# A state-space scan and a channel mixer on one core: decays folded into B and C, small matmuls packed into the array

## The chip, the cores and the metric

The kernel runs on one core of a Trainium2 chip. The metric is the device time of one execution in microseconds (us). The kernel before takes 431.71 us, the median of three runs (431.37 to 436.95). In a core, TensorE (PE) multiplies matrices: it loads a stationary operand (PEld) and streams a moving one past it, with results in PSUM, which has eight banks. VectorE (DVE), ScalarE (ACT) and GpSimd (POOL) work element by element, and SyncE's queue (SPq) issues the DMAs. An engine executes its own instructions in order and waits on semaphores for the others.

## The reference

Two blocks, one after the other. The first is a scan over 768 tokens, in 4 batches and 8 heads, with 32 channels per head (d) and 16 state numbers (n):

```
log_a = np.log(np.clip(a, 1e-06, 1.0))
for c in range(nc):                                  # chunks of 32 tokens
    cum = np.cumsum(la, axis=-1)
    L = np.exp(cum[:, :, :, None] - cum[:, :, None, :]) * causal
    M = np.einsum('bhin,bhjn->bhij', Cc, Bc) * L
    y_intra = np.einsum('bhij,bhjd->bhid', M, xc)
    y_inter = np.einsum('bhin,bhnd->bhid', Cc, state) * np.exp(cum)[:, :, :, None]
    y[:, :, sl] = y_intra + y_inter
    Bx = np.einsum('bhjn,bhjd->bhjnd', Bc, xc) * np.exp(cum[:, :, -1:] - cum)[:, :, :, None, None]
    state = np.exp(np.sum(la, axis=-1))[:, :, None, None] * state + np.sum(Bx, axis=2)
```

The second is a mixer on y as x, of shape (4, 768, 256), with U (768 x 32), V (32 x 768), w_ch1 (256 x 1024) and w_ch2 (1024 x 256), all four given as float64:

```
h = x.transpose(0, 2, 1) @ U @ V
u = x + h.transpose(0, 2, 1)
return u + np.maximum(u @ w_ch1, 0.0) @ w_ch2
```

## The kernel before

Everything is fp32. The scan goes in chunks of 128 tokens, six to a batch, with all eight heads at once. `scan_front` (lines 206 to 249) prepares a chunk. GpSimd spreads log a into `lau`; TensorE transposes B, C times its decay, and C (L225); C is masked into four copies (CTm, L230) so that one matmul with 64 rows and 512 columns gives C B^T of four heads (L248, two per chunk, one for each half of the rows, each into a PSUM bank of its own). The decay matrix L comes from a matmul of `lau` with a 0/1 triangle (L239, two per chunk of 512 columns), an exp on ScalarE (L240) and a mask on GpSimd (L241); VectorE multiplies both into M (L249). `scan_back` (lines 251 to 280) makes y, token-major, in one bank: one matmul of the state with the decayed C (L259) and eight matmuls, one per head, with M as the stationary operand and 32 moving columns (L262). Then come the sum of new states, as one 128 x 256 matmul (L269), its masking on VectorE (L272), the old state's decay on GpSimd (L276) and their sum (L279).

The mixer of a batch is a list of pieces (lines 283 to 342). `project` makes U^T y in six matmuls of 256 columns (L292) and VectorE copies the result to pT (L294). `u_channel_major` (four times) transposes three blocks of y (L299) and adds V's product of 32 rows and 384 columns in the same bank (L302), which VectorE copies (L304). `up` (16 times) is two matmuls of 384 columns (L311) and a relu on VectorE or ScalarE (L314, L316). `down` (six times) is a V product (L323), eight matmuls of 256 columns (L325) and an addition of y on VectorE (L327). A DMA writes three token blocks at a time.

The weights' float64 words are taken apart on chip by `to_fp32` (lines 164 to 200): eleven tiles (U one, V two, w1 four, w2 four), each with seven operations on VectorE (lines 179 to 191, and L196) and two on GpSimd (L194, L198). Their words land in six buffers. The DMA queue brings the first batch's B, C and x first, then the weights, then the other batches.

Order of the work: the loop at the end gives the scan of batch 0 the weight tiles as pieces, and the scan of every later batch the mixer of the batch before; the last mixer runs alone. Written order is only a wish here: a scheduler places the instructions on each engine, TensorE included. An instruction that stands behind a waiting one on its engine waits too.

Of the kernel before, what the change touches and what calls it, by code (L numbers as in the profile page):

```python
# [10 lines left out]
INT32 = mybir.dt.int32  # L11
WCOLS = 512
NWORDS = 6
AF = mybir.ActivationFunctionType
ALU = mybir.AluOpType


@with_exitstack
def kernel(
# [26 lines left out]
    NC = S // P  # L46
    DM = NH * D
# [6 lines left out]
    assert NH * N == P and DM == 2 * P and HS % P == 0  # L54

    const = ctx.enter_context(tc.tile_pool(name="const", bufs=1))
    raw = ctx.enter_context(tc.tile_pool(name="raw", bufs=NB * NC))
# [5 lines left out]
    BANKS = {"misc": 1, "diff": 2, "g": 2, "y": 1, "mlp": 2}  # L63
# [11 lines left out]
    x_sb, bc_sb = {}, {}  # L75

    def load(b, c):
        sl = ts(c, P)
        bc = bc_sb[b, c] = raw.tile([P, 2, NH, N], FP32, tag="bc", name="bc")
        nc.sync.dma_start(out=bc[:, 0], in_=B[b, :, sl, :].rearrange("h s n -> s h n"))  # L80
        nc.sync.dma_start(out=bc[:, 1], in_=C[b, :, sl, :].rearrange("h s n -> s h n"))
        xt = x_sb[b, c] = raw.tile([P, NH, D], FP32, tag="x", name="x")
        nc.sync.dma_start(out=xt, in_=x[b, :, sl, :].rearrange("h s d -> s h d"))

    for c in range(NC):
        load(0, c)
# [3 lines left out]
    V_sb = const.tile([RK, S], FP32)  # L90
# [4 lines left out]
    def load_words(dst, src):  # L95
        """dst [p, i, j], and its float64 words in DRAM, [p, i, (j two)]."""
        p, i, j = dst.shape
        t = raw.tile([P, 2 * WCOLS], INT32, tag="words", name="words", bufs=NWORDS)
        t = t[:p, :2 * i * j].rearrange("p (i j) -> p i j", i=i)
        nc.sync.dma_start(out=t, in_=src)  # L100
        weights.append((dst, t))
# [3 lines left out]
    for k in range(2):  # L105
        load_words(V_sb[:, None, ts(k, S // 2)], V2[:, None, ts(k, S)])
    for c in range(NCB):
        for k in range(DF // WCOLS):
            load_words(w1[:, c, None, ts(k, WCOLS)],
                       w12[ts(c, P), None, ts(k, 2 * WCOLS)])  # L110
# [4 lines left out]
    for b in range(1, NB):  # L115
        for c in range(NC):
            load(b, c)

# [5 lines left out]
    upto = const.tile([P, P], FP32)  # L124
    nc.gpsimd.affine_select(
        out=upto, in_=ones, pattern=[[1, P]], compare_op=ALU.is_ge, fill=0.0,
        base=0, channel_multiplier=-1)
    after = const.tile([P, P], FP32)
    nc.gpsimd.affine_select(
        out=after, in_=ones, pattern=[[-1, P]], compare_op=ALU.is_ge, fill=0.0,  # L130
        base=-1, channel_multiplier=1)
    hmask = const.tile([P, NH], FP32)
    nc.gpsimd.affine_select(
        out=hmask, in_=ones[:, :NH], pattern=[[-N, NH]], compare_op=ALU.is_ge, fill=0.0,
        base=0, channel_multiplier=1)
    nc.gpsimd.affine_select(
        out=hmask, in_=hmask, pattern=[[N, NH]], compare_op=ALU.is_ge, fill=0.0,
        base=N - 1, channel_multiplier=-1)
    tmask = const.tile([P, 4], FP32)
    nc.vector.tensor_tensor(out=tmask, in0=hmask[:, 0:4], in1=hmask[:, 4:8], op=ALU.add)  # L140

# [1 line left out]
    la = const.tile([P, NB, NC, NH], FP32)  # L143
    R = NB * NH * NC // 2
    la_ps = bank("misc", 2, R)
# [11 lines left out]
    decay = const.tile([P, 3, NB, NC, NH], FP32)  # L157
    for k, tri in enumerate((upto, after, ones)):
        d = bank("diff", NB * NC * NH)
        nc.tensor.matmul(out=d, lhsT=tri, rhs=la_flat, start=True, stop=True)  # L160
        nc.scalar.activation(decay[:, k].rearrange("p b c h -> p (b c h)"), d, AF.Exp)

# [1 line left out]
    def to_fp32(dst, words):  # L164
        """dst = the float32 nearest to each float64, of which words hold the low and high half.

        A float64 is +-2^(e - 1023) (1 + h 2^-20 + l 2^-52): the factor in brackets is rounded to
        float32 once, and the power, clamped to float32's range, put together as bits.
        """
        p, i, j = dst.shape  # L170
        words = words.rearrange("p i (j two) -> p (i j) two", two=2)
# [218 lines left out]
```

## Time and profile before

| | us |
|---|---|
| median of three runs | 431.71 |
| runs | 431.37, 431.71, 436.95 |
| span of the profiled execution | 433.4 |
| PE busy in it | 400.8 (92%), 1552 matmul records |
| DVE busy | 163.3 (38%) |
| ACT busy, POOL busy | 64.2, 91.7 |

The profiled execution's own time is its span of 433.4 us from the first to the last instruction, 1.7 us above the median of the runs. An fp32 matmul appears as two records of a load and two of a matmul, a transpose as one of each; a few records can be missing. A matmul's time in a row includes its drain, so that in a dense stretch the distance from start to start is what it costs. TensorE's clock has two levels, 1.2 and 2.4 GHz; PEclk is the granted share of the higher one.

### The profile page before, as it was taken

How to read it: one execution, taken by the hardware profiler on the slowest of the kernel's cores; microseconds unless marked ns; L12 is line 12 of the kernel's file. 1: busy time of each engine (PE TensorE's matmuls, PEld its weight loads, DVE VectorE, ACT ScalarE, POOL GpSimd, SP SyncE). 2: the span in 40 equal slices, each digit the busy share in tenths (PEclk: the TensorE clock that was granted, in tenths of full speed). 3: DMA queues.
4: the chain of work that ended last, by engine and by line, in shares of the span. 5: the costliest groups of instructions: out<-in, count | busy, mean ns of one | idle time of the engine just before them, and what ended most of it. 6: DMA issues, size and time to landing. Idle time of an engine off the chain costs nothing.

```text
span 433.4 us, 4009 instructions
## 1 busy us (share of the span) xinstructions
PE 400.8 (92%) x1552; PEld 250.8 (58%) x1552; DVE 163.3 (38%) x315; ACT 64.2 (15%) x134; POOL 91.7 (21%) x120
## 2 busy tenths in 40 slices
PE   6297975959999999999999999999999999999996
PEld 3063542545356775575558656755666667657664
DVE  2279789675333224313341343132323230211110
ACT  4112101101111112110220122011301210010000
POOL 4347746333100202202220222022111100000000
PEclk9769688575589999999999999996999999979999
DMA  7965999500000010010000100000000100100101
GB/s 96 207 154 103 159 117 116 66 2 0 0 1 2 0 37 2 0 38 0 0 2 0 36 2 0 5 32 1 2 0 0 38 0 0 38 0 0 38 0 36
DMA packets 80850, 14.37 MB, mean 33 GB/s; under 512 B 75968, under 2 KB 79232, under 8 KB 80832
## 3 DMA queue, kind: packets, MB, share of 16 engines
q1 hardware_dynamic: 80832, 14.13, 18.0%
q8 instruction: 12, 0.20, 0.2%
q14 instruction: 6, 0.05, 0.0%
HBM read 10.98 MB, written 3.15 MB: 33 GB/s over the span
## 4 chain that ended last, share of the span: by engine, by line
PE 85%; DVE 8%; SPq 3%; issue 2%; DMA 1%; POOL 1%; ACT 0%; DVEq 0%
PE mlp L311 20%; PE mlp L325 20%; PE y L262 11%; PE diff L239 7%; PE g L248 7%; PE mlp L302 4%; PE mlp L323 3%; PE misc L269 2%; PE y L259 2%; PE mlp L292 2%; PE mlp L299 2%; PE misc L225 2%; DVE f L196 1%; DVE M L249 1%; DVE cdec L215 1%
## 5 line engine op out<-in xcount | busy, mean ns | idle before, releaser
L311 PE MATMUL mlp<-uT,w 128*128 128x384 f32 x256 | 92.7, 508 | 0.0
L325 PE MATMUL mlp<-w,gT 128*128 128x256 f32 x384 | 90.1, 386 | 0.0
L325 PEld LDWEIGHTS mlp<-w,gT 128*128 128x128 f32 x384 | 70.7, 190 | 18.8 <-issue 10.2
L311 PEld LDWEIGHTS mlp<-uT,w 128*128 128x128 f32 x256 | 48.9, 197 | 42.3 <-issue 16.0
L262 PEld LDWEIGHTS y<-x,M 128*128 128x128 f32 x384 | 56.2, 226 | 5.3 <-issue 3.1
L262 PE MATMUL y<-x,M 128*128 128x32 f32 x384 | 55.0, 302 | 0.0
L239 PE MATMUL diff<-lau,after 128*128 128x512 f32 x96 | 54.8, 675 | 0.1
L241 POOL TENSOR_SCALAR_AFFINE_SELECT L<-L 128x512 f32<-128x512 f32 x48 | 33.7, 706 | 82.7 <-ACT L L240 82.6
L249 DVE TENSOR_TENSOR M<-g,L 128x512 f32<-128x512 f32 x48 | 31.1, 685 | 35.6 <-PE g L248 32.3
L327 DVE TENSOR_TENSOR o<-mlp,ytok 128x256 f32<-128x256 f32 x24 | 10.2, 424 | 84.3 <-PE mlp L325 84.3
L276 POOL TENSOR_TENSOR kept<-state,decay 128x256 f32<-128x256 f32 x16 | 11.3, 708 | 142.5 <-DVE state L279 113.9
L248 PE MATMUL g<-CTm,T 64*128 64x512 f32 x96 | 32.5, 760 | 7.9 <-DVE CTm L230 7.9
L240 ACT ACTIVATE L<-diff 128x512 f32<-128x512 f32 x48 | 28.2, 597 | 47.0 <-PE diff L239 27.1
L314 DVE TENSOR_SCALAR gT<-mlp 128x384 f32<-128x384 f32 x32 | 17.8, 555 | 42.0 <-PE mlp L311 41.9
L316 ACT ACTIVATE gT<-mlp 128x384 f32<-128x384 f32 x32 | 15.7, 491 | 116.5 <-PE mlp L311 116.5
L265 ACT COPY ytok<-y 128x256 f32<-128x256 f32 x24 | 9.0, 373 | 153.2 <-PE y L262 153.2
L210 POOL TENSOR_SCALAR_AFFINE_SELECT lau<-la 128x1024 f32<-128x1024 f32 x24 | 27.2, 1136 | 6.1 <-PE diff L239 3.5
L225 PE MATMUL misc<-ident,bc 128*128 128x128 f32 x48 | 13.8, 306 | 13.9 <-DVE state L272 13.2
L239 PEld LDWEIGHTS diff<-lau,after 128*128 128x128 f32 x96 | 18.9, 220 | 10.6 <-issue 6.8
L272 DVE TENSOR_TENSOR state<-misc,hmask 128x256 f32<-128x256 f32 x20 | 8.4, 422 | 42.6 <-PE misc L269 42.6
L225 PEld LDWEIGHTS misc<-ident,bc 128*128 128x128 f32 x48 | 7.6, 159 | 26.7 <-DVE state L272 22.3
L248 PEld LDWEIGHTS g<-CTm,T 64*128 64x128 f32 x96 | 8.5, 216 | 21.6 <-DVE CTm L230 17.1
(57 smaller groups left out, 285.0 us busy)
## 6 DMA issues: line engine op xcount, KB each, us to landing
words<-in_moe_w_ch_dram SPq DMA_DIRECT2D x8, 512.0 KB, 3.8
x<-in_x_dram SPq DMA_DIRECT2D x24, 128.0 KB, 3.4
out_dram<-o SPq DMA_DIRECT2D x8, 384.0 KB, 2.5
bc<-in_B_dram SPq DMA_DIRECT2D x24, 64.0 KB, 3.1
bc<-in_C_dram SPq DMA_DIRECT2D x24, 64.0 KB, 2.8
words<-in_moe_U_dram SPq DMA_DIRECT2D x1, 192.0 KB, 4.0
words<-in_moe_V_dram SPq DMA_DIRECT2D x2, 96.0 KB, 3.8
a_sb<-in_a_dram SPq DMA_DIRECT2D x1, 96.0 KB, 2.1
```

What stands on the lines that cost most here:

```text
L210: nc.gpsimd.affine_select(out=lau, in_=la[:, b, c, :, None].to_broadcast([P, NH, P]), pattern=[[0, NH], [1, P]], compare_op=ALU.is_ge, fil ...
L225: nc.tensor.transpose(out=tp[:, k], in_=src.rearrange("p h n -> p (h n)"), identity=ident)
L239: nc.tensor.matmul(out=d, lhsT=after, rhs=lau[:, hs], start=True, stop=True)
L240: nc.scalar.activation(L[:, hs], d, AF.Exp)
L241: nc.gpsimd.affine_select(out=L[:, hs], in_=L[:, hs], pattern=[[0, 4], [1, P]], compare_op=ALU.is_ge, fill=0.0, base=0, channel_multiplier=-1)
L248: nc.tensor.matmul(out=g, lhsT=T[r, 0], rhs=CTm[r], start=True, stop=True)
L249: nc.vector.tensor_tensor(out=M[:, hs], in0=g, in1=L[:, hs], op=ALU.mult)
L262: nc.tensor.matmul(out=y[:, ts(h, D)], lhsT=s["M"][:, h], rhs=xt[:, h], start=(c == 0 and h == 0), stop=True, skip_group_check=True)
L302: nc.tensor.matmul(out=t, lhsT=pT[:, ts(n, P)], rhs=V_sb[:, ts(k, HS)], start=False, stop=True, skip_group_check=True)
L311: nc.tensor.matmul(out=g, lhsT=w1[:, n, ts(m, P)], rhs=uT[:, n, ts(k, HS)], start=(n == 0), stop=(n == NCB - 1))
L314: nc.vector.tensor_relu(gT[k][:, m], g)
L325: nc.tensor.matmul(out=o, lhsT=gT[k][:, m, ts(j, P)], rhs=w2[:, m], start=False, stop=(m == NM - 1))
```

## The change

The scan goes in pairs of chunks. Its decays are factored: exp(cum_i - cum_j) becomes a factor on C's row i times one on B's row j, relative to one of two reference tokens in the chunk (FB and FC, made once for all chunks; `v` counts the references). `prep` forms the scaled B and C of a pair (Bs on VectorE, Cs and bd on GpSimd), each head taking 32 numbers (2 x 16); `turn` transposes them, four transposes a chunk; L, `lau`, the exp and their masks are gone, and M is C B^T with a causal bit mask. `gram` (C B^T) packs four heads into four 32-row tiles of the array, with a PSUM bank each; `state` and the inner part of `ychannel` pack four heads into four 32-column tiles; `project` does the same with four token blocks of U, whose result stands in four row groups for which V is loaded four times over (V4). y is made channel-major, which is what the mixer's up-product takes; `ytokens` transposes it to token-major for `project` alone. `mixed` adds h to y in place with one matmul of 128 rows; `down` starts from two transposes of u in place of V's product and y's addition. The PSUM banks are 3 for everything (w), 4 for C B^T, 1 for y. `to_fp32` has five operations on VectorE, one on ScalarE and one on GpSimd. TensorE's order is the written one (`manual_schedule`); the other engines' orders still come from the scheduler.

The core of the diff:

```
-        for k in range(2):
-            hs = slice(4 * k, 4 * k + 4)
-            d = bank("diff", 4, P)
-            nc.tensor.matmul(out=d, lhsT=after, rhs=lau[:, hs], start=True, stop=True)
-            nc.scalar.activation(L[:, hs], d, AF.Exp)
...
-            g = bank("g", 4, P)
-            nc.tensor.matmul(out=g, lhsT=T[r, 0], rhs=CTm[r], start=True, stop=True)
-            nc.vector.tensor_tensor(out=M[:, hs], in0=g, in1=L[:, hs], op=ALU.mult)
...
+    def turn(k, c):
+        tp = bank("w", 4, P)
+        for i, name in enumerate(("Bs", "Cs")):
+            flat = s[name].rearrange("p h v n -> p (h v n)")
+            for g in range(2):
+                nc.tensor.transpose(out=tp[:, 2 * i + g], in_=flat[:, ts(2 * c + g, P)],
+                                    identity=ident)
...
+    def gram(k):
+        g_ps = bank("g", 4, 2, 2, P)
+        for c in range(2):
+            T = s["T", c]
+            for g in range(2):
+                for r in range(4):
+                    rows = ts(r, Q)
+                    nc.tensor.matmul(out=g_ps[:, r, c, g], lhsT=T[rows, g], rhs=T[rows, 2 + g],
+                                     start=True, stop=True, skip_group_check=True)
+        for c in range(2):
+            nc.vector.tensor_tensor(
+                out=M[:, :, c].bitcast(INT32), in0=g_ps[:, :, c].bitcast(INT32),
+                in1=causal[:, None, None, :].to_broadcast(sh), op=ALU.bitwise_and)
+    def state(k):
...
+        for c in range(n):
+            for g in range(2):
+                for r in range(4):
+                    h = 4 * g + r
+                    nc.tensor.matmul(
+                        out=A[ts(r, Q), c, g],
+                        lhsT=s["bd"][:, c * NH + h].rearrange("p v n -> p (v n)"),
+                        rhs=x_sb[k][:, c, h], start=r not in first, stop=True,
+                        skip_group_check=True)
...
+    def ychannel(k):
...
+                nc.tensor.matmul(
+                    out=y[:, c, g], lhsT=wide[:, g].rearrange("p r d -> p (r d)"),
+                    rhs=s["T", c][:, 2 + g], start=fresh, stop=False, skip_group_check=True)
...
+        for c in range(2):
+            for g in range(2):
+                for r in range(4):
+                    nc.tensor.matmul(
+                        out=y[ts(r, Q), c, g], lhsT=x_sb[k][:, c, 4 * g + r],
+                        rhs=s["M"][:, r, c, g], start=False, stop=True, skip_group_check=True)
...
         def project():
+            for c in range(NC):
+                nc.tensor.matmul(out=p[ts(c % 4, Q)], lhsT=U_sb[:, c], rhs=ytok[b][:, c],
+                                 start=(c < 4), stop=(c >= NC - 4), skip_group_check=True)
+            nc.scalar.copy(out=pT, in_=p)
...
+        def mixed(k, n):
+            h = bank("w", HS)
+            nc.tensor.matmul(out=h, lhsT=pT[:, ts(n, P)], rhs=V4[:, ts(k, HS)],
+                             start=True, stop=True)
+            u = uT[:, n, ts(k, HS)]
+            nc.vector.tensor_tensor(out=u, in0=h, in1=u, op=ALU.add)
...
         def down(k, j):
-            nc.tensor.matmul(out=o, lhsT=V_sb[:, ts(t, P)], rhs=pT, start=True, stop=False)
+            for n in range(NCB):
+                nc.tensor.matmul(out=o[:, ts(n, P)], lhsT=uT[:, n, ts(HT * k + j, P)], rhs=ident,
+                                 is_transpose=True, start=(n == 0), stop=False,
+                                 skip_group_check=True)
...
-            nc.vector.tensor_tensor(out=hold[k][:, j], in0=o, in1=xs[:, t], op=ALU.add)
+            nc.scalar.copy(out=hold[k][:, j], in_=o)
...
+    with tc.manual_schedule(engines={PE}):
...
+            if k + 2 < last:
+                prep(k + 2)
+            if k + 1 < last:
+                turn(k + 1, 0)
+                some(parts[0])
+                turn(k + 1, 1)
...
+            some(parts[1])
+            ychannel(k)
+            if k + 1 < last:
+                state(k + 1)
+                gram(k + 1)
+            some(parts[2])
```

`some(n)` takes the next n pieces: weight tiles in batch 0, pieces of the mixer of the batch before in the later ones (22 for three pairs; `project` and the four `mixed` run at the start of a batch).

TensorE's order in the middle of a batch, before: L259 and L262 are y of a chunk, L269 its states, L239 and L225 belong to the next chunk, L248 is its C B^T, and L311 and L325 are the mixer's up and down.

```order
L259 MATMUL y<-state,T 128x256
L262 MATMUL y<-x,M 128x32 x8
L269 MATMUL misc<-x,bdec 128x256
L239 MATMUL diff<-lau,after 128x512
L225 MATMUL misc<-ident,bc 128x128
L225 MATMUL misc<-ident,cdec 128x128
L225 MATMUL misc<-ident,bc 128x128
L239 MATMUL diff<-lau,after 128x512
L311 MATMUL mlp<-uT,w_104 128x384
L248 MATMUL g<-CTm,T 128x512 x2
L311 MATMUL mlp<-uT,w_104 128x384 x7
```

The same place after: L298 is `turn`, L368 and L375 are `ychannel`, L331 `state`, L311 `gram`, L386 `ytokens`, L419 the mixer's up.

```order
L298 MATMUL w<-ident,Bs 128x128 x2
L298 MATMUL w<-ident,Cs 128x128 x2
L419 MATMUL w<-yT,w_98 128x384 x4
L368 MATMUL y<-T,wide 128x128 x4
L375 MATMUL y<-M,x 32x128 x16
L331 MATMUL w<-x,bd_260 32x32 x16
L311 MATMUL g<-T 128x128 x16
L431 MATMUL w<-ident,yT 128x128 x2
L435 MATMUL w<-w_99,gT 128x256 x8
```

The two 512-column products of a chunk are gone, and the scan's part of a pair now stands as three runs of 16 small matmuls in a row, with the mixer's pieces before and behind them and no longer between them.

VectorE's order in the first batch, before: L179 to L196 take weight tiles apart, L249 is M, and L272 evacuates the sum of states.

```order
L249 TENSOR_TENSOR M<-g,L 128x512 x2
L185 SCALAR_TENSOR_TENSOR power<-words,power 128x512
L196 SCALAR_TENSOR_TENSOR f<-l,f 128x512
L179 TENSOR_SCALAR power<-words 128x512
L188 TENSOR_SCALAR h<-words 128x512
L181 TENSOR_SCALAR power<-power 128x512
L191 TENSOR_SCALAR l<-words 128x512
L183 TENSOR_SCALAR power<-power 128x512
L196 SCALAR_TENSOR_TENSOR f<-l,f 128x512
L185 SCALAR_TENSOR_TENSOR power<-words,power 128x512
L272 TENSOR_TENSOR state<-misc,hmask 128x256
```

After, in the same stage: L237 to L248 take weight tiles apart, L345 adds the states, L316 masks M, L388 copies y's tokens.

```order
L275 TENSOR_TENSOR Bs<-bc,FB 128x512
L248 SCALAR_TENSOR_TENSOR rest<-words,power 128x512
L345 SCALAR_TENSOR_TENSOR S<-S,kept,w 128x32 x2
L316 TENSOR_TENSOR M<-g,causal 128x4x256 x2
L237 TENSOR_SCALAR e<-words 128x512
L244 TENSOR_SCALAR top<-words 128x512
L237 TENSOR_SCALAR e<-words 128x512
L244 TENSOR_SCALAR top<-words 128x512
L241 SCALAR_TENSOR_TENSOR power<-words,power 128x512
L388 COPY ytok<-w 128x512
```

Weight tiles still stand between the scan's operations on VectorE, two at a time, and the states are now added behind fewer of them.

## Rows read from the trace of the kernel before

**Rows 1.** The page: its first line, and the granted clock in 40 slices.

```profile
span 433.4 us, 4009 instructions
PEclk9769688575589999999999999996999999979999
```

**Rows 2.** Stretches: us, busy time (and instructions) of PE, PEld, DVE, ACT, POOL, PEclk, DMA share, GB/s.

```profile
80.00:90.00 10.00, 6.15 (x12) 1.60 (x8) 8.43 (x11) 1.08 (x2) 4.93 (x5) 0.76 0.18 22
...
100.00:110.00 10.00, 10.00 (x27) 5.85 (x28) 5.13 (x9) 1.84 (x4) 3.94 (x4) 0.50 0.00 0
...
140.00:160.00 20.00, 20.00 (x89) 14.01 (x88) 5.45 (x11) 2.40 (x6) 2.89 (x4) 1.00 0.06 20
```

**Rows 3.** Timeline of the front: start, duration, engine, line, operation [idle before <-releaser].

```profile
18.58 0.26 DVE L179 TENSOR_SCALAR power<-words 128x192 int32<-128x192 int32 x1 [8.75 <-DMA words<-in_moe_U_dram]
...
73.03 0.41 DVE L272 TENSOR_TENSOR state<-misc,hmask 128x256 f32<-128x256 f32 x1
...
81.47 1.22 PE L269 MATMUL misc<-x,bdec 128*128 128x256 f32 x2
...
90.11 0.41 DVE L272 TENSOR_TENSOR state<-misc,hmask 128x256 f32<-128x256 f32 x1
...
102.99 0.41 DVE L294 COPY pT<-mlp 32x256 f32<-32x256 f32 x1
```

**Rows 4.** Timeline of PE, one chunk of the scan in the settled stage.

```profile
145.62 0.59 PE L259 MATMUL y<-state,T 128*128 128x256 f32 x2
146.06 1.87 PE L262 MATMUL y<-x,M 128*128 128x32 f32 x16
...
149.13 0.27 PE L225 MATMUL misc<-ident,bc 128*128 128x128 f32 x1
149.24 0.27 PE L225 MATMUL misc<-ident,cdec 128*128 128x128 f32 x1
...
150.41 0.69 PE L323 MATMUL mlp<-pT,V_sb 32*128 32x256 f32 x2
...
151.67 1.13 PE L248 MATMUL g<-CTm,T 64*128 64x512 f32 x4
```

**Rows 5.** Timeline of PE, mixer: channel-major steps of batch 1, up and down of batch 3.

```profile
201.15 0.55 PE L299 MATMUL mlp<-ident,ytok 128*128 128x128 f32 x3
...
202.47 0.55 PE L299 MATMUL mlp<-ident,ytok 128*128 128x128 f32 x3
...
405.89 10.48 PE L311 MATMUL mlp<-uT,w 128*128 128x384 f32 x32
416.30 0.69 PE L323 MATMUL mlp<-pT,V_sb 32*128 32x256 f32 x2
416.93 3.72 PE L325 MATMUL mlp<-w,gT 128*128 128x256 f32 x16
420.58 0.69 PE L323 MATMUL mlp<-pT,V_sb 32*128 32x256 f32 x2
```

**Rows 6.** Timeline: a load and its matmul behind a wait, and out of the queue.

```profile
66.57 0.50 PEld L239 LDWEIGHTS diff<-lau,after 128*128 128x128 f32 x2 [0.86 <-issue]
66.60 2.48 PE L239 MATMUL diff<-lau,after 128*128 128x512 f32 x4
...
79.45 0.51 PEld L248 LDWEIGHTS g<-CTm,T 64*128 64x128 f32 x4
79.46 2.08 PE L248 MATMUL g<-CTm,T 64*128 64x512 f32 x4
```

**Rows 7.** Groups by line and form on VectorE: count | busy us, mean ns of one | idle before.

```profile
L249 DVE TENSOR_TENSOR M<-g,L 128x512 f32<-128x512 f32 x48 | 31.1, 685 | 35.6 <-PE g L248 32.3 <-POOL L L241 3.3
...
L185 DVE SCALAR_TENSOR_TENSOR power<-words,power 128x512 int32<-128x512 int32 x8 | 6.3, 790 | 0.0
...
L179 DVE TENSOR_SCALAR power<-words 128x512 int32<-128x512 int32 x8 | 5.1, 634 | 0.0
```

**Rows 8.** Stretches, columns as in rows 2, behind the last batch's scan.

```profile
378.00:381.00 3.00, 3.00 (x7) 1.31 (x7) 1.12 (x2) 0.00 (x0) 0.00 (x0) 0.55 0.00 0
```

More of the change, by code (lines that the diff above doesn't have):

```diff
@@ L46 @@
     NC = S // P
+    NPR = NC // 2
     DM = NH * D
@@ L113 @@
                    w22[m * P:(m + 2) * P].rearrange("(m p) d -> p m d", p=P))
-    for b in range(1, NB):
-        for c in range(NC):
-            load(b, c)
+    for k in range(NPR, NB * NPR):
+        load(k)
     ident = const.tile([P, P], FP32)
@@ L123 @@
     nc.vector.memset(ones, 1.0)
[L124 to L140, printed above, removed]
+    def triangle(name, out, pattern, base, mult, in_=None):
+        nc.gpsimd.affine_select(
+            out=out, in_=ones[:, :out.free_size()] if in_ is None else in_, pattern=pattern,
+            compare_op=ALU.is_ge, fill=0.0, base=base, channel_multiplier=mult)
+        return out
@@ new lines @@
+    upto = triangle("upto", const.tile([P, P], FP32, name="upto"), [[1, P]], 0, -1)
+    after = triangle("after", const.tile([P, P], FP32, name="after"), [[-1, P]], -1, 1)
+    low = [triangle("low", const.tile([P, P], FP32, name=f"low{v}"), [[0, P]], 31 + 64 * v, -1)
+           for v in range(2)]
+    high = const.tile([P, P], FP32)
+    nc.vector.tensor_tensor(out=high, in0=ones, in1=low[0], op=ALU.subtract)
+    ref = [const.tile([P, P], FP32, name=f"ref{v}") for v in range(2)]
+    nc.vector.tensor_tensor(out=ref[0], in0=upto, in1=low[0], op=ALU.subtract)
@@ new lines, in state @@
+    def state(k):
+        b, q = pairs[k]
+        s = st[k]
+        n = 2 if q < NPR - 1 else 1
+        A = bank("w", 2, 2, D)
+        first = set()
+        for c in range(n):
[7 more added lines that the diff above has]
+                        skip_group_check=True)
+                    first.add(r)
+        for c in range(n):
+            j = 2 * q + c
+            new = att.tile([P, 2, D], FP32, tag="S", name="S", bufs=3)
+            if j == 0:
+                nc.vector.tensor_copy(out=new, in_=A[:, c])
+            else:
+                old = st["S", b, j]
+                for g in range(2):
+                    nc.vector.scalar_tensor_tensor(
+                        out=new[:, g], in0=old[:, g], scalar=kept[:, b, j, g, None],
+                        in1=A[:, c, g], op0=ALU.mult, op1=ALU.add)
+            st["S", b, j + 1] = new
+            wide = att.tile([P, 2, 4, D], FP32, tag="wide", name="wide", bufs=4)
+            nc.gpsimd.tensor_tensor(
+                out=wide, in0=new[:, :, None, :].to_broadcast(wide.shape),
+                in1=rmask[:, None, :, None].to_broadcast(wide.shape), op=ALU.mult)
+            st["wide", b, j + 1] = wide
@@ L283, in mixer, with ytokens @@
+    def ytokens(k):
+        b, q = pairs[k]
+        t = bank("w", 2, 2, P)
+        for c in range(2):
+            for g in range(2):
+                nc.tensor.transpose(out=t[:, c, g], in_=yT[b][:, g, ts(2 * q + c, P)],
+                                    identity=ident)
+        nc.vector.tensor_copy(
+            out=ytok[b][:, 2 * q:2 * q + 2].rearrange("p c (g d) -> p c g d", g=2), in_=t)
+        st.pop(k)
+        x_sb.pop(k)
     def mixer(b):
-        xs = ytok[b]
-        uT = mix.tile([P, NCB, S], FP32, tag="uT", name="uT")
@@ L342, in mixer, with some @@
         return pieces
-    order = [(b, c) for b in range(NB) for c in range(NC)]
-    scan_front(*order[0])
-    pieces = [lambda w=w: to_fp32(*w) for w in weights]
-    for i, (b, c) in enumerate(order):
-        if c == 0 and b:
-            pieces = mixer(b - 1)
-        if i + 1 < len(order):
-            scan_front(*order[i + 1])
-        n = -(-len(pieces) // (NC - c))
-        for f in pieces[:n]:
-            f()
-        pieces = pieces[n:]
-        scan_back(b, c)
-    for f in mixer(NB - 1):
-        f()
+    with tc.manual_schedule(engines={PE}):
+        last = len(pairs)
+        prep(0)
+        turn(0, 0)
+        turn(0, 1)
+        state(0)
+        gram(0)
+        prep(1)
+        pieces = [lambda w=w: to_fp32(*w) for w in weights]
+        for k in range(last + 1):
+            b, q = divmod(k, NPR)
+            def some(n):
+                for _ in range(min(n, len(pieces))):
+                    pieces.pop(0)()
+            if k:
+                ytokens(k - 1)
+            if q == 0 and b:
+                some(len(pieces))
+                pieces = mixer(b - 1)
+                some(5)
+            if k == last:
+                break
+            quota = -(-len(pieces) // (NPR - q))
+            parts = [quota // 3, quota // 3, quota - 2 * (quota // 3)]
+            if k + 2 < last:
[4 more added lines that the diff above has]
+                turn(k + 1, 1)
+            else:
+                some(parts[0])
+            some(parts[1])
[4 more added lines that the diff above has]
+            some(parts[2])
+        some(len(pieces))
 _INS = ['x', 'a', 'B', 'C', 'moe_U', 'moe_V', 'moe_w_ch1', 'moe_w_ch2']
```

279 lines of the change are left out of this document (148 added, 131 removed).

## The prediction

> **What bounds the kernel now.** I read the page's slices first. The granted clock [rows 1] is mixed for the first third of the span and nearly full afterwards; the table of stretches [rows 2] says why. From 80 to 90 us VectorE is busy 8.43 of 10 us and TensorE 6.15; from 100 to 110 TensorE works, but at the lower clock (0.50 of 2.4 GHz, so 1.2); from 140 to 160 it is busy 20.00 of 20 at 1.00. So there are two stages with two limits. Until about 103 us, when pT of batch 0 is copied [rows 3], VectorE's own order sets the pace: it takes the weights apart and serves the scan in one queue. The state sum A of one chunk is on TensorE at 81.47 [rows 3], but its evacuation (L272) starts at 90.11, behind two weight tiles' operations; the same operation of the chunk before started at 73.03, so a chunk takes 17.1 us there. After that TensorE never waits, and the time is the sum of what it executes. A microsecond taken off TensorE's settled work is a microsecond off the span; in the front, only VectorE's queue counts.
>
> The span is 433.4 us [rows 1], 1.7 above the median of the runs shown (431.71); I work in the span and take 1.7 off at the end.
>
> **TensorE per chunk, before.** Start to start in the settled stage [rows 4]: y from the state at 145.62 to the next mixer matmul at 150.41 is 4.79 us, and the two C B^T products (L248) are 1.06 more (1.13 with their drain): 5.85 us a chunk, 11.7 a pair. Prices in there: a transpose 0.11 (149.13 to 149.24); the eight y products (L262) with 128-column weights and 32 moving columns 1.87 with their drain, so about 0.21 each, which is the weight load and not the columns. Columns cost about 1.7 ns each: 384 take 0.65 and 256 take 0.456 (10.41 us for 16 and 3.65 for 8 [rows 5]), so 128 take 0.21 by estimate.
>
> **Do small tiles run side by side?** The L248 row says yes for two row tiles: four records of 512 columns last 1.13 us, where one 512-column matmul alone (two records) needs 0.87 by the column price; in turn they would need 1.74. So two 64-row halves overlap fully, with about 0.2 for entering and leaving the mode. Four row tiles (gram) and four column tiles (y, states, U) are not in this trace. Bounds for the 16 matmuls of one kind in a pair: side by side, four rounds of 0.21 = 0.85 us; one after the other, 16 x 0.21 = 3.4 (states, 32 columns, 0.85).
>
> **What is late next: issue.** y, states and gram of a pair are 48 matmuls, 192 records (each fp32 matmul is two loads and two passes) in a row. Where TensorE's sequencer has just waited, the load starts at 66.57 and its matmul at 66.60; where they stood in the queue, 79.45 and 79.46 [rows 6]. I take the 0.03 us as the price of issuing one record. 192 x 0.03 = 5.8 us; I take off 1.0 for records that are queued while the matmuls ahead still run (a choice; no row has it), so 4.8 us a pair, 3.8 where the next pair sums one state. Below this is the overlapped 0.85 + 0.85 + 0.2 plus three mode changes at 0.2 = 2.5 us; above it, tiles in turn, 3.4 + 3.4 + 0.9 = 7.7. I choose 4.8, nearest to the rows on overlap and issue.
>
> The Trainium skill (TensorE: Matmul & The Clock Gate, section "Wait — 56ns, not 53.3ns?") puts the floor from start to start at about 25 ns per matmul, whatever its size. By it, if weight loads issue beside the matmuls, the 96 matmul records of a pair would take 2.4 us; no run here shows such a stream, and the row's 31 ns between a load and its matmul speaks for counting both. That is rival A below, priced there from rows.
>
> **Sum of TensorE after, in the settled stage.** Scan: eight pairs' y + states + gram at 4.5 on average = 36; the last pair's y alone 1.2; eight pairs' turns (8 transposes, 0.88) = 7; nine pairs' ytokens (4 transposes) = 4; 30 wide products at 0.21 = 6.4; mode changes 9 x 0.3 = 2.7. Together 57 us, against 18 chunks x 5.85 = 105.
>
> Mixer of a batch, before [rows 5]: project, six 256-column matmuls, 2.7; four channel-major steps at 1.32 (201.15 to 202.47) = 5.3; up 2 x 10.41 = 20.8; six downs at 4.28 (416.30 to 420.58) = 25.7; sum 54.5. After: project in column tiles, two rounds of 256 columns and a mode change, 1.2 (2.7 if in turn); mixed, four 384-column matmuls with all 128 rows, 2.6; up unchanged 20.8; down with two transposes in place of the 0.63 of the V product (416.30 to 416.93), 0.22 + 3.65 = 3.87, times six 23.2. Sum 47.8, plus 1.5 for waits at the start of a batch (transpose, copy by VectorE, project, copy by ScalarE, mixed: three hand-overs of about 0.5 that TensorE's fixed order doesn't fill). 49.3 x 4 = 197. So 57 + 197 = 254 us.
>
> What else moves is off this path at 100% TensorE: the exp of L, two masks of L on GpSimd, CTm go; Bs, Cs, bd, wide come, some 4 us a pair on GpSimd and 5 on VectorE against a pair's share of 28 us (254 / 9). The cover goes only if TensorE waits for M: the two masks (1,024 columns each, 1.37 by twice L249 [rows 7]) delay a relu behind them by 2.7 us, and the three PSUM banks bridge about that. The output add moves from VectorE to a ScalarE copy: nothing.
>
> **The front.** A weight tile costs VectorE seven operations now, from 0.63 to 0.79 us (lowest and highest of the seven groups [rows 7]), about 5.1 us; after, five, about 3.6, plus one on ScalarE; GpSimd loses one of two. Eight big tiles: 41 to 29; U and V (now 128 rows, same columns) some 10 to 6. The scan's own on VectorE: per chunk M 1.37, CTm 0.7 and about 1.7 of small ones, 3.8, so 23 for six; after, per pair Bs 0.7, M 2.7, states 0.8, token copy 0.7, so 4.9, and four pairs lie ahead of the first mixer = 20. Total 74 to 55 us. The first weight is taken apart at 18.58 us, when it has landed [rows 3], so the 84 us from there to 103 were 74 of work (some 5 of it done before) and waits; in the same ratio 55 gives 60 to 63. So pT at about 78 us instead of 103. Bounds: 62 if the waits on TensorE (which is at 1.2 GHz there) go with its shorter chain; 95 if the new hop over ScalarE or the fourfold load of V (0.6 MB more) stalls each tile.
>
> From there: 78 + 254 (less 1.2 for project) + about 4 for project and mixed at 1.2 GHz, twice as long + 4.3 from the last matmul to the end as now (three downs from 416.30 end at 429.1; 433.4). Sum 339; less 1.7, and rounded, **338 us**.
>
> **Rivals.**
> A, issue is no bound: 2.9 instead of 4.5 for the blocks (with their drains), 8 x 1.6 = 13 less, and the front at its low end, up to 16 less: 310 to 325, say 318. For it: a queued load and its matmul start 0.01 us apart [rows 6]. Against: the queue has to be filled first.
> B, column tiles run in turn, row tiles side by side: y 3.4 and the rest as before, about 1.4 more per pair x 9, project 1.5 x 4, so 338 + 19 = 357; with row tiles in turn too, 369. For it: the one column-tiled operation of the trace, project, shows no overlap, but it uses one tile only.
> C, the clock falls after each block. At 378 to 381 us the granted clock is 0.55 [rows 8], at the end of the last batch's y products, project and K = 32 products, which stand in a row in the code. A block here is some 6 us of small tiles with dense work around it. Three us at half clock lose 1.5 us of work; if two such stretches follow each block, 9 x 3 = 27, so 365.
> D, slower: the array drains at each change of tile, not only of mode. Then each of 48 matmuls pays its own passes (0.21, states 0.05) and about 0.21 of drain (L248's excess): 32 x 0.42 + 16 x 0.26 = 17.6 us a pair against 4.8, 8.5 x 12.8 = 109 more: 447. It decides from about 0.25 us extra a matmul. L248's two tiles side by side speak against it, and only for row tiles. The Trainium skill (TensorEngine Tiling (Array Packing), section "Key Properties") says that changing the mode, not just the tile, drains the engine; the 0.63 us step from a K = 32 product to the next matmul, against 0.456 for its columns, agrees for the mode.
> E, gains eaten by waits in the fixed order: TensorE can't pass a late operand any more. To lose everything, each of 27 block starts would have to wait 3.5 us; that ends at no change, 432.
>
> **Chances.** Forecast 0.45, A 0.22, B 0.14, C 0.13, D 0.03, E 0.03. The measurement can tell about 2%. Faster by over 2%: the first four, 0.94; within 2%: 0.03; slower: 0.03. The range takes A's low end and C or B with a late front: 306 to 374.
>
> **What would show it.** Right: y, states and gram of a pair in some 4 to 6 us, records about 0.03 apart; pT at 70 to 85 us; down 3.9 us each; TensorE at 100% from the first up on, with the clock at 1.00. Column tiles in turn would show as y records 0.1 apart. The prediction is wrong if TensorE idles in the settled stage ahead of y or project, if the clock is at 0.5 for long after 90 us, or if pT comes after 95.

## The result and the profile after

The changed kernel takes 304.17 us (median of 4, 303.6 to 304.41) against 432.51 us of the kernel before (median of 4, 431.37 to 436.95): a ratio of 0.705, 95% interval 0.701 to 0.708. On a second chip it took 304.89 us, ratio 0.700 (0.697 to 0.704). The forecast of 338 us was 34 too high, and the time lies 2 us below its range: faster, as forecast, but by more than the prediction allowed. Its rival A (318) was nearer, and still 14 too high.

The page of the kernel after, its first lines, the granted clock and the queue that brings instructions:

```profile
span 301.9 us, 4870 instructions
...
PE 258.4 (86%) x2094; PEld 194.6 (64%) x2094; DVE 113.8 (38%) x201; ACT 58.5 (19%) x115; POOL 53.2 (18%) x69
...
PEclk9755967756999999999999999999999999999999
...
q8 instruction: 16, 0.26, 0.4%
```

The clock is mixed for ten of 40 slices (75 us; twelve and 130 us before, [rows 1]) and then stays up, also behind the blocks of small tiles and in the last mixer, where it fell before [rows 8]. Stretches of the kernel after, columns as in [rows 2]:

```profile
20.00:30.00 10.00, 6.96 (x111) 6.12 (x112) 9.40 (x21) 3.19 (x6) 3.58 (x5) 0.54 0.91 293
30.00:40.00 10.00, 3.85 (x91) 2.99 (x89) 10.00 (x17) 3.66 (x6) 2.64 (x2) 0.97 0.51 131
...
60.00:70.00 10.00, 2.55 (x7) 1.07 (x8) 9.33 (x16) 1.09 (x2) 5.39 (x5) 0.50 1.03 109
...
140.00:160.00 20.00, 20.00 (x180) 15.98 (x179) 6.08 (x11) 3.81 (x8) 3.23 (x5) 1.00 0.00 1
```

The same two stages: DVE is full until the first mixer can start, then TensorE is. TensorE's timeline in the front, answering to the copy of pT in [rows 3]:

```profile
52.46 0.64 PE L403 MATMUL w<-ytok,U_sb 128*32 128x256 f32 x8
66.98 1.07 PE L403 MATMUL w<-ytok,U_sb 128*32 128x256 f32 x4 [13.88 <-DVE ytok L388]
68.52 5.31 PE L409 MATMUL w<-V,pT 128*128 128x384 f32 x8 [0.47 <-ACT pT L405]
```

`project` stands in TensorE's order for 13.88 us, until DVE, which has weights ahead of it, copies the last tokens. pT (the result of `project`) is ready at 68.5 us; before, its copy began at 102.99. A pair in the settled stage and the start of a batch, answering to [rows 4, 5]:

```profile
116.23 1.08 PE L375 MATMUL y<-M,x 128*32 128x128 f32 x32
117.13 0.48 PE L331 MATMUL w<-x,bd 128*32 128x32 f32 x32
117.54 1.17 PE L311 MATMUL g<-T 32*128 32x128 f32 x32
118.64 0.44 PE L431 MATMUL w<-ident,yT 128*128 128x128 f32 x2
118.91 3.62 PE L435 MATMUL w<-w,gT 128*128 128x256 f32 x16
122.37 0.38 PE L431 MATMUL w<-ident,yT 128*128 128x128 f32 x2
...
131.10 0.63 PE L403 MATMUL w<-ytok,U_sb 128*32 128x256 f32 x4 [0.21 <-DVE ytok L388]
132.20 2.85 PE L409 MATMUL w<-V,pT 128*128 128x384 f32 x8 [0.47 <-ACT pT L405]
134.88 0.38 PE L298 MATMUL w<-ident,Bs 128*128 128x128 f32 x2
```

From start to start: y's 16 products with M 0.90 us, states 0.41, C B^T 1.10, together 2.41 us a pair. A down is 3.67 from one pair of transposes to the next (126.04 less 122.37), as against 4.28 before.

Where the 131.5 us between the two spans (433.4 and 301.9) came from: the front until pT is there, and behind it, for each part, the sum of the distances from one start to the next on TensorE:

| part | before | after | gain, us |
|---|---|---|---|
| until pT of batch 0 | 102.9 | 68.5 | 34.4 |
| the scan's products | 99.8 | 38.5 | 61.3 |
| project (3), channel-major steps or `mixed` (4 batches) | 34.6 | 19.1 | 15.5 |
| 24 downs and the end | 106.5 | 92.5 | 14.0 |
| ups | 89.6 | 83.3 | 6.3 |

The ups are the same products in both, so most of their 6.3 us is the clock's. In all parts together the clock is worth more than that; columns as in [rows 2], the kernel before and then the kernel after, behind pT:

```profile
103.00:433.00 330.00, 326.17 (x1314) 207.73 (x1314) 90.92 (x187) 45.76 (x98) 40.36 (x56) 0.95 0.03 10
```

```profile
68.50:302.00 233.50, 227.28 (x1668) 169.83 (x1668) 60.37 (x105) 40.43 (x84) 20.94 (x26) 0.99 0.11 22
```

Before, the granted clock is 0.50 from 103 to 122 us, 0.69 from 290 to 301 and 0.66 from 378 to 388, which costs 16 us; after, it is 0.54 from 68.5 to 74 and 1.00 from there on, which costs 2.5. So some 14 of the 97 us gained behind the front are the clock's and not the shorter work's. No run took the clock apart.

### The profile page after: what moved, and what is told of

The parts are those of the page before. It is cut to its first block, busy times and chain, and to the rows that moved or that the text cites. A ratio compares the mean times of both kernels' runs of the same rounds, so it can differ in the third digit from the quotient of the medians.

```text
span 301.9 us, 4870 instructions
## 1 busy us (share of the span) xinstructions
PE 258.4 (86%) x2094; PEld 194.6 (64%) x2094; DVE 113.8 (38%) x201; ACT 58.5 (19%) x115; POOL 53.2 (18%) x69
## 4 chain that ended last, share of the span: by engine, by line
PE 77%; DVE 10%; SPq 5%; DMA 3%; issue 1%; POOL 1%; ACT 1%; DVEq 0%; POOLq 0%
PE w L419 28%; PE w L435 27%; PE w L409 5%; PE y L375 4%; PE g L311 3%; PE y L368 3%; PE w L298 2%; SPq L93 2%; DVE M L316 2%; PE w L431 2%; DMA words<-in_moe_U_dram 2%; DVE rest L248 2%; SPq L94 2%; SPq L97 1%; DVE top L244 1%
## 5 line engine op out<-in xcount | busy, mean ns | idle before, releaser
L419 PE MATMUL w<-yT,w 128*128 128x384 f32 x256 | 86.9, 489 | 0.0
L435 PE MATMUL w<-w,gT 128*128 128x256 f32 x384 | 86.9, 379 | 0.0
L435 PEld LDWEIGHTS w<-w,gT 128*128 128x128 f32 x384 | 71.1, 190 | 8.7
L419 PEld LDWEIGHTS w<-yT,w 128*128 128x128 f32 x256 | 47.3, 190 | 29.3
L422 DVE TENSOR_SCALAR gT<-w 128x384 f32<-128x384 f32 x32 | 17.8, 557 | 64.0 <-PE w L419 64.0
L275 POOL TENSOR_TENSOR Cs<-bc,FC 128x512 f32<-128x512 f32 x12 | 16.4, 1364 | 78.5 <-issue 46.1
L316 DVE TENSOR_TENSOR M<-g,causal 128x1024 int32<-128x1024 int32 x24 | 28.3, 1217 | 3.1 <-PE g L311 3.0
L424 ACT ACTIVATE gT<-w 128x384 f32<-128x384 f32 x32 | 15.7, 491 | 55.3 <-PE w L419 55.3
L388 DVE COPY ytok<-w 128x512 f32<-128x512 f32 x12 | 8.2, 683 | 31.4 <-PE w L386 31.4
L275 DVE TENSOR_TENSOR Bs<-bc,FB 128x512 f32<-128x512 f32 x12 | 10.8, 897 | 23.7 <-PE w L298 14.6
L345 DVE SCALAR_TENSOR_TENSOR S<-S,kept,w 128x32 f32<-128x32 f32 x32 | 6.3, 243 | 32.1 <-PE w L331 17.0
L375 PE MATMUL y<-M,x 128*32 128x128 f32 x384 | 14.4, 289 | 4.6 <-DVE M L316 4.6
L298 PE MATMUL w<-ident,Bs 128*128 128x128 f32 x48 | 10.6, 307 | 9.0 <-DVE Bs L275 9.0
L311 PE MATMUL g<-T 32*128 32x128 f32 x384 | 15.9, 308 | 0.0
L298 PEld LDWEIGHTS w<-ident,Bs 128*128 128x128 f32 x48 | 7.1, 161 | 12.9 <-DVE Bs L275 9.0
L375 PEld LDWEIGHTS y<-M,x 128*32 128x32 f32 x384 | 10.2, 114 | 7.2 <-DVE M L316 5.9
L368 PEld LDWEIGHTS y<-T,wide 128*128 128x128 f32 x80 | 11.8, 212 | 4.3 <-POOL wide L350 1.9
```

The lines of the kernel that those rows point to most:

```text
L275: eng.tensor_tensor(out=t, in0=bc[:, i].rearrange("p c h n -> p (c h) n")[:, :, None, :].to_broadcast(shape), in1=F[:, b, cs].rearrange("p ...
L298: nc.tensor.transpose(out=tp[:, 2 * i + g], in_=flat[:, ts(2 * c + g, P)], identity=ident)
L311: nc.tensor.matmul(out=g_ps[:, r, c, g], lhsT=T[rows, g], rhs=T[rows, 2 + g], start=True, stop=True, skip_group_check=True)
L316: nc.vector.tensor_tensor(out=M[:, :, c].bitcast(INT32), in0=g_ps[:, :, c].bitcast(INT32), in1=causal[:, None, None, :].to_broadcast(sh), ...
L368: nc.tensor.matmul(out=y[:, c, g], lhsT=wide[:, g].rearrange("p r d -> p (r d)"), rhs=s["T", c][:, 2 + g], start=fresh, stop=False, skip_g ...
L375: nc.tensor.matmul(out=y[ts(r, Q), c, g], lhsT=x_sb[k][:, c, 4 * g + r], rhs=s["M"][:, r, c, g], start=False, stop=True, skip_group_check= ...
```

## The experiments

Times of the runs are compared with 304.2 to 304.9 us of the kernel after; each ratio is to the kernel before on the same chip. The expectations of the first three runs count up to 24 pairs; there are twelve, three a batch, and nine of them lie behind the first project.

**Tiles in turn.** In `gram`, `state` and the inner products of y the tile becomes the outermost loop, so that consecutive matmuls go to the same tile. The arithmetic and the number of records stay.

```
-        for c in range(2):
-            for g in range(2):
-                for r in range(4):
+        for r in range(4):
+            for c in range(2):
+                for g in range(2):
```

> Theory T (the four tiles overlap, and a pair's blocks are short because of it): with consecutive matmuls on one tile, y, states and C B^T run one after the other. The 32 products with M and the 32 of C B^T have 128 columns or 128 stationary columns each, about 0.106 us per step of 128 columns at full clock by y's block (0.9 us for 8 full matmuls and 8 steps of four), so y goes from 0.9 to 0.85 + 32 x 0.053 = 2.55 to 4.2 us, C B^T from 1.1 to 1.7 to 3.4 us, states from 0.40 to 0.45 to 0.85 us: 2.3 to 6.0 us more a pair, over 21 pairs at full clock 48 to 126 us at most, and I take the lower end: time 350 to 360 us. Rival P (packing plays no part, records are issued one by one and the issue sets the blocks): 304 us, within 1%.

331.2 us, ratio 0.761 (0.757 to 0.766): 27 us more. One pair of this run, with one state summed, from y to the next up:

```profile
247.78 2.13 PE L375 MATMUL y<-M,x 128*32 128x128 f32 x29
...
250.29 2.82 PE L311 MATMUL g<-T 32*128 32x128 f32 x32
253.04 4.14 PE L419 MATMUL w<-yT,w 128*128 128x384 f32 x12
```

From 247.78 to 253.04 are 5.26 us, against 2.24 for the same pair of after (102.52 to 104.76 in its timeline). 3.0 us in each of eight pairs and 1.5 in the last are 26 of the 27 us. So packing is where the block's shortness comes from, and issue alone (rival P) is not the bound. C B^T takes 2.75 us in turn and 1.10 packed: a factor of 2.5, not of 4.

**Only y in turn.** The same edit in y's products alone.

> Only the products of y with M in turn of their column tiles. Theory T: y's block of a pair from 0.9 to 2.55 to 4.2 us, the rest as it is: 22 to 50 us more over the scan's pairs, the lower end more likely, 326 to 332 us. Rival P (issue sets the blocks): 304 us. The rival B of the prediction, that column tiles run one after the other whatever the order, would leave the time at 304 too, and y's block at what it is.

319.28 us, ratio 0.734 (0.729 to 0.738): 15 us more. In the last pair, where nothing of the scan follows, y's 32 records stand alone:

```profile
252.36 2.46 PE L375 MATMUL y<-M,x 128*32 128x128 f32 x32
254.75 0.44 PE L431 MATMUL w<-ident,yT 128*128 128x128 f32 x2
```

2.39 us in turn, 0.90 packed. So rival B of the prediction (column tiles run one after the other anyhow) is shown wrong, in size too: its 3.4 us is not reached even in turn.

**Eight times the states' records.** The state products are issued eight times over, each time starting the sum anew.

```
-        for c in range(n):
+        for rep in range(8):
+          first.clear()
+          for c in range(n):
```

> Each of a pair's state matmuls (32 outputs) is issued eight times with the same result: 224 more matmuls, 448 more records of loads and products a pair. Price of the prediction, 0.03 us a record: 13.4 us more a pair, at 24 pairs (18 with all 32, 6 with 16) 280 us more at most where TensorE's block stands alone, 500 to 580 us. Theory I (a record costs at most 0.008 us, as the states' block of after, 0.40 us for 64 records, allows): 3.6 us a pair or less, 304 + 75 = 380 us as the upper end; if the columns set it instead (32 columns at 2.4 GHz, four tiles at once), 0.75 us a pair, 320 us.

345.0 us, ratio 0.793 (0.788 to 0.798). The page counts 9,350 instructions, 4,480 more than after; the 40.8 us more are 9 ns for each, against the 30 of the prediction (134 us). A states' block of this run and its instruction queue over the whole run:

```profile
237.30 2.14 PE L333 MATMUL w<-x,bd 128*32 128x32 f32 x229
241.51 0.44 PE L333 MATMUL w<-x,bd 128*32 128x32 f32 x27 [2.07 <-issue]
241.88 2.09 PE L311 MATMUL g<-T 32*128 32x128 f32 x32
```

```profile
q8 instruction: 34, 0.56, 0.6%
```

229 matmul records with as many loads go out in 2.14 us, the drain of the last included: at most 4.7 ns a record, 9.3 ns from one matmul record to the next. Then TensorE stands for 2.07 us, and the profile shows nothing that it waits for. Such halts of the states' block are 20.4 us in all, so about half of the 9 ns. In a window around this block (236 to 246 us) the only transfers are two packets of the instruction queue, 0.03 MB; the first lands at 239.95, and TensorE goes on at 241.51. Each of the eight halts of this kind behind 80 us ends 1.2 to 1.6 us after such a packet has landed. That the instructions had run out is therefore the likely reading, though no run tested it. A stream of small matmuls has two prices, 5 ns a record and these halts; at the rate of the kernel after, 192 records a pair with long products between, no wait of TensorE is put down to issue behind 80 us.

**TensorE's order left to the scheduler.**

```
-    with tc.manual_schedule(engines={PE}):
+    if True:
```

> The order of TensorE's instructions left to the scheduler instead of the program's order, nothing else changed. Theory F (the fixed order is one of the causes: blocks of a pair in a row, one mixer piece between them, so no wait in the settled stage): the scheduler's order splits blocks and brings waits, 3 to 15% slower, 313 to 350 us. Rival S (the fixed order is worth nothing, the arithmetic is): 304 us within 2%, with the same block times. I take S.

301.18 us, ratio 0.691 (0.688 to 0.695): a little faster, about 3 us of 304. The first start of a mixer in the settled stage of this run:

```profile
128.68 0.64 PE L403 MATMUL w<-ytok,U_sb 128*32 128x256 f32 x8
129.25 0.71 PE L368 MATMUL y<-T,wide 128*128 128x128 f32 x4
129.89 0.41 PE L403 MATMUL w<-ytok,U_sb 128*32 128x256 f32 x2
129.92 0.41 PE L375 MATMUL y<-M,x 128*32 128x128 f32 x4
130.13 0.39 PE L403 MATMUL w<-ytok,U_sb 128*32 128x256 f32 x2
130.35 0.60 PE L375 MATMUL y<-M,x 128*32 128x128 f32 x6
130.99 2.85 PE L409 MATMUL w<-V,pT 128*128 128x384 f32 x8
```

The scheduler puts y of the next pair into the two hand-overs of project. Of the waits of 80 to 300 us, 2.0 us in six places in after, 0.7 in two are left. The fixed order is no part of the gain. The waits are 1.3 of its 3 us; what the rest is was not taken apart: here y of a pair already stands in the front's wait, and the first batch's `mixed` products take 2.7 us for 5.1, at the higher clock, while pT comes 2.2 us later (70.77 for 68.52).

**The old conversion in the kernel after.** Its `to_fp32` is replaced by the one of the kernel before (seven operations on DVE, two on POOL).

> The conversion of the kernel before (seven DVE operations a tile in place of five, as the listing of before has them) in the kernel after. Theory D (between 20 and 67 us DVE's queue sets the end of the front, 46 of 47 us busy): 8 conversion tiles of w and the ones of U and V stand in that queue, about 1.5 to 2 us of DVE work more each: 10 to 17 us more, 314 to 321 us. Rival M (the weights' transfers set it, DMA 95 to 103% busy from 40 to 80 us): under 4 us, at most 308 us.

312.64 us, ratio 0.724 (0.716 to 0.732): 8 us more, below the 10 to 17. The last part of project and the step behind it:

```profile
77.40 1.07 PE L408 MATMUL w<-ytok,U_sb 128*32 128x256 f32 x4 [14.67 <-DVE ytok L393]
78.93 1.65 PE L414 MATMUL w<-V,pT 128*128 128x384 f32 x2 [0.47 <-ACT pT L410]
```

pT comes 10.4 us later (78.93 for 68.52). So DVE's queue sets the front, and the conversion is 8 to 10 of the front's 34.4 us. The rest would be the scan's lighter work there; no run took that apart.

**Down from V's product, with 128 rows and with 32.** Instead of the two transposes and the copy:

```
+            nc.tensor.matmul(out=o, lhsT=V4[:, ts(HT * k + j, P)], rhs=pT, start=True, stop=False,
+                             skip_group_check=True)
...
+            nc.vector.tensor_tensor(out=hold[k][:, j], in0=o, in1=ytok[b][:, HT * k + j],
+                                    op=ALU.add)
```

and in the second run `V4[:RK, ...]` and `pT[:RK]`, 32 rows each, which leaves three of the four groups of partial sums of U^T y out of the product.

> Down from a product of V with U^T y over all 128 rows, and y added on DVE, instead of two transposes of u and a copy. Two passes of 256 columns at 0.216 us (3.46 us for 16 such records) against two transposes of 128 columns at 0.107: 0.22 us a tile, 24 tiles: 5.2 us more, 309.4 us. Theory K (a change between 32-row and 128-row products costs time of its own, and no such change is here): 309 us. Rival N (the column count alone): the same, 309 us. This run is the reference for the next one.

> As the run before it, but the product takes 32 rows of V and of U^T y alone, as the kernel before did; here three of the four groups of partial sums of U^T y are left out of it. Theory K (each change between 32-row and 128-row products costs time of its own): before's rows give 4.27 us from one product to the next where after has 3.67, so 0.6 us a tile, 24 tiles: 14.4 us more than after, 318.5 us, 9 us above the run with 128 rows. Rival N (only columns count): as that run, 309 us.

308.88 us (ratio 0.715, 0.709 to 0.722) and 316.95 us (0.734, 0.727 to 0.742). With 128 rows, then with 32:

```profile
185.85 0.59 PE L430 MATMUL w<-pT,V 128*128 128x256 f32 x2
186.28 3.62 PE L433 MATMUL w<-w,gT 128*128 128x256 f32 x16
189.74 0.59 PE L430 MATMUL w<-pT,V 128*128 128x256 f32 x2
```

```profile
189.09 0.69 PE L430 MATMUL w<-pT,V 32*128 32x256 f32 x2
189.72 3.72 PE L433 MATMUL w<-w,gT 128*128 128x256 f32 x16
193.37 0.69 PE L430 MATMUL w<-pT,V 32*128 32x256 f32 x2
```

The columns are the same, but a down takes 3.89 us in the one and 4.28 in the other: 0.20 on the way into the 32-row product's successor (0.63 for 0.43) and 0.19 inside the eight large products (3.65 for 3.46). Theory K holds: going in and out of the 32-row mode costs 0.39 us a down, 9.4 over 24 by rows and 8.1 in the times.

**The kernel before with the new down alone** (the two transposes and the copy in its `down`).

> The kernel before with the new down alone: two transposes and a copy on ACT instead of the product of 32 rows and the addition on DVE. Theory K: 4.27 us from one down to the next becomes 3.67, 24 of them on TensorE's path: 14 us less than before, 418 to 420 us. Rival (before's settled stage is bound by what the pair's chain waits for, so TensorE's saving is idle time): within 2% of before, 426 us or more.

416.43 us, ratio 0.957 (0.950 to 0.965): 18 us less, 4 more than expected. Downs, and a stretch behind the last batch's scan, columns as in [rows 2]:

```profile
399.00 0.38 PE L324 MATMUL mlp<-ident,uT 128*128 128x128 f32 x2
399.22 3.62 PE L328 MATMUL mlp<-w,gT 128*128 128x256 f32 x16
402.68 0.38 PE L324 MATMUL mlp<-ident,uT 128*128 128x128 f32 x2
```

```profile
366.00:369.00 3.00, 3.00 (x11) 1.63 (x12) 1.11 (x2) 0.12 (x1) 0.00 (x0) 1.00 0.00 0
```

The page of this run has no lower clock in the second half, where [rows 1] has a 6 and a 7:

```profile
PEclk9859786565559999999999999999999999999999
```

The stretch of the kernel before that answers to the one at 366 us stands in [rows 8]; the two that follow there:

```profile
381.00:384.00 3.00, 3.00 (x6) 1.69 (x5) 0.00 (x0) 0.49 (x1) 0.00 (x0) 0.50 0.00 0
384.00:388.00 4.00, 4.00 (x12) 2.26 (x11) 0.56 (x1) 0.49 (x1) 0.00 (x0) 0.86 0.00 0
```

Of the 19.1 us between the two spans (433.4 and 414.3), 24 x 0.61 = 14.6 are the downs. The clock gives another 6.8: 3 us at 0.55, 3 at 0.50 and 4 at 0.86 lose 3.4 us before, the fall behind the third batch's scan (11 us at 0.69, from 290) 3.4 more, and neither is here. Against them, pT comes 1.9 us later (its copy begins at 104.89, before at 102.99). Why the clock fell in the one and not in the other was not tried.

**The second weight among the ups.** Its four tiles are converted behind project and mixed of the first batch.

```
+        late = [lambda w=w: to_fp32(*w) for w in weights[-(NM // 2):]]
...
+                for i, f in enumerate(late):
+                    pieces.insert(2 * i + 2, f)
```

> The conversion of the second weight's four tiles moved behind the first batch's project and mixed, among its ups. Theory D (DVE's queue sets the end of the front; some 3.5 us of DVE work a tile stand ahead of the operation that project waits for): project starts 6 to 14 us earlier, 290 to 298 us. Rival M (the transfers set it): the first down then waits for the last tile that lands near 80 us, and the time stays within 2%, 300 to 305 us. Third, if the mixer's evacuations on DVE now stand behind conversions: slower, up to 310 us.

297.96 us, ratio 0.691 (0.686 to 0.697): 6 us less. Project's last part:

```profile
60.03 1.07 PE L403 MATMUL w<-ytok,U_sb 128*32 128x256 f32 x4 [9.40 <-DVE ytok L388]
61.58 4.40 PE L409 MATMUL w<-V,pT 128*128 128x384 f32 x8 [0.47 <-ACT pT L405]
```

6.95 us earlier than in after, and nearly all of it arrives at the end. Theory D again, now from the other side.

**Both together, and an addition moved to DVE.** The kernel after once more; the free order with the late weight; and that with the last addition of a conversion on DVE (`nc.vector` for `nc.gpsimd`).

> The changed kernel itself once more, beside the runs that follow: 304 us, ratio 0.705 within 1%.

> The scheduler's order of TensorE and the late conversion of the second weight together. If the two take time out of different stretches: 304.2 - 3 - 6 = 295 us. If both only bring project forward (DVE's queue sets both): as the late conversion alone, 298 us. Rival: the free order puts ups ahead of the weight that now comes later, and the first mixer waits: over 301 us.

> As the run before it, but the last addition of a conversion on DVE instead of POOL. Theory L (DVE and POOL lock each other out: in after DVE's operations of 0.41 to 0.68 us take 1.1 to 1.75 us where a POOL operation runs beside them): each addition of 1.3 to 1.6 us on POOL costs DVE about 1.0, on DVE itself 0.6: 0.4 us less for each of some 12 conversions ahead of project: 2 to 5 us less than the run before it. Rival Q (each queue by itself): 12 x 0.6 = 7 us more than the run before it, as DVE's queue sets the front.

304.89 us (0.700, 0.697 to 0.704), 297.68 us (0.684, 0.681 to 0.688) and 297.06 us (0.683, 0.679 to 0.686). The last two beat both kernels; against each other their intervals overlap. The two gains don't add up. With both, project's result is there 2.3 us earlier than with the late weight alone (59.25 for 61.58), but TensorE then waits behind it for DVE and ACT, 4.7 us in four places up to 85 us (0.9 in one place with the late weight alone); the longest:

```profile
82.39 1.56 PE L419 MATMUL w<-yT,w 128*128 128x384 f32 x4 [2.59 <-DVE ytok L388]
```

One group on DVE from 30 to 60 us, first with the addition on POOL, then on DVE:

```profile
L244 DVE TENSOR_SCALAR top<-words 128x512 int32<-128x512 int32 x6 | 5.6, 930 | 0.0
```

```profile
L244 DVE TENSOR_SCALAR top<-words 128x512 int32<-128x512 int32 x4 | 2.2, 551 | 0.0
```

The same operation takes 930 ns on average beside POOL's additions and 551 without them. This group changes most; over the whole run the five operations of a 512-column tile together are 0.85 us shorter on DVE, and the addition there takes 0.85. So an addition on POOL does cost DVE time, and moving it to DVE costs as much again: neither theory L's 2 to 5 us nor Q's 7 is seen. The Trainium skill (SBUF — State Buffer, section "SBUF: two separate sides") states that VectorE and GpSimd share a pair of ports which the one that starts first holds for its whole instruction; on VectorE's side this concerns operations in a two-port mode or with two inputs in SBUF. The two rows agree, though no run shows the mode of this operation.

## Why the prediction was wrong, point by point

**Two stages, the settled one bound by TensorE's sum: right.** No wait ahead of y, 20.00 of 20 us busy, and nearly every microsecond put on TensorE's settled work in the experiments came out at the end (26 by rows and 27 in the time with tiles in turn, 9.4 and 8.1 with 32 rows for 128).

**The step that failed: the price of issue.** The prediction read the 0.03 us between a load and its matmul behind a wait [rows 6] as the price of issuing one record, and made 4.8 us of a pair's 192 records (4.5 on average). The blocks take 2.41 (2.3 on average): over eight pairs 17 of the 37 us by which the span was overestimated (339 for 301.9). The repeated states show at most 4.7 ns a record. The row was misread: the idle time in it is that of the loads alone. In the kernel before, the product ahead of it runs, with its drain, until 66.59:

```profile
65.53 1.06 PE L292 MATMUL mlp<-ytok,U_sb 128*32 128x256 f32 x2
```

The load began at 66.57, while that product still drained, and the matmul followed it at 66.60, so 0.03 us is no price of a record. Where all of TensorE had waited, in the kernel after, the first load of project's last part and its first matmul start at the same hundredth.

```profile
131.10 0.14 PEld L403 LDWEIGHTS w<-ytok,U_sb 128*32 128x32 f32 x4 [0.70 <-DVE ytok L388]
```

The queued pair right under the misread row of [rows 6] (0.01 us) already spoke against 0.03 us. The lower bound, 0.85 + 0.85 + 0.2 and some for modes (2.5), was nearly the true value. By the Trainium skill's floor of 25 ns a matmul (TensorE: Matmul & The Clock Gate, section "Wait — 56ns, not 53.3ns?"), named in the prediction, 96 matmul records are 2.4 us, an estimate that happens to be the block's time; but at most 9.3 ns from start to start in the repeated states show that such a floor doesn't hold for small fp32 matmuls spread over four tiles. The block's time is near that of its columns side by side and its changes of mode.

**Mode changes, 2.7 us on top of the blocks: wrong.** The blocks' distances hold them already; y and states share a mode.

**Down 3.87: too high.** The eight large products were taken at 3.65, as in [rows 5], but 0.19 of that was the return from the 32-row mode, which goes too: 3.67, 24 x 0.2 = 4.6 us. The price of a mode change was in the prediction, and was left out of this term.

**Waits at a batch's start 1.5 us: too high.** 0.21 and 0.47 in the rows, 0.7 in all: about 3 us.

**The front, pT at 78: right in kind, 10 us off in size.** DVE's queue sets it, as the old conversion and the late weight show. DVE's work was sized right (53.4 us until 68.5, forecast 55). The prediction scaled the old waits along with it (55 us of work gave 60 to 63); in fact the waits went, and DVE is busy for 48.1 of the 49.9 us from 18.6 to 68.5. That is the lower bound (62) more than the middle.

Together 17 + 2.7 + 4.6 + 3 + 10 = 37, the whole miss. Five terms, all of them too high; two smaller ones cancel (the wide products took 7.5 us for 6.4, the lower clock cost 2.5 for 4).

**From span to time, less 1.7: wrong in sign.** Every run's time is 1.7 us more than its span (303.6 for 301.9). By that the profiled execution of the kernel before took 435.1 us and was longer than the median run. The span of 339 meant 341 us, and the miss is 37 in the times too.

**Rivals.** A was right in its mechanism (issue is no bound) and, with the front at its low end, comes to 310; the terms for modes, downs and waits were too dear in it as well. B fell by the run with only y in turn; C and D fell by the clock at 1.00 and the blocks at 2.4 us. E fell in size: the waits behind 80 us are 2.0 in all.

## What to carry to other kernels

Pack small fp32 matmuls by letting consecutive ones go to different tiles: on this chip the order of the loops alone is worth 27 us of 331. Take a price of issue from a stream of records, never from one load and its matmul, and look first whether the product ahead of them is still at work; and when an operation in another mode leaves, take its drain out of the neighbours' rows too. Where one queue of an element-wise engine sets a front, look at what stands in it that the end of the front doesn't need: moving four weight tiles behind it gave 6 us.

## What was not expected of the hardware

A run of small matmuls may outrun its own instructions: after 229 matmul records and as many loads at 4.7 ns a record TensorE stood for 2.07 us, and this halt and seven others end within 1.6 us of an instruction packet's landing. The number of packets, 34 in this run and 16 in after, only follows the number of instructions (9,350 and 4,870). And four tiles are not four times as fast as one: y's products in turn on a tile take 2.39 us for 0.90 packed, C B^T 2.75 for 1.10. By the columns' price sixteen products one after the other would take 3.4 us, so neighbours on one tile must overlap in part; the runs don't show how.
